# One layer of a fused kernel on one Trainium2 core: the tiles of its second product are put between the steps of its first

## The chip, the cores and the metric

The kernel runs on one core of one Trainium2 chip. The metric is the device time of one execution in microseconds (us). The time given for a kernel is the median of several executions; beside it there is one profiled execution, from which all rows below come. TensorE (PE) multiplies matrices, ScalarE (ACT) and VectorE (DVE) work element by element, and SyncE (SP) issues the DMAs.

## The reference

```python
attn = softmax(mask(q @ k.T / 8))  @ v      # window of 64, 4 x 8 heads, 576 x 64
x = attn as [2304, 512]
h = relu(x @ w_in1);  x2  = h * h @ w_out1            # layer 1: 512 -> 2048 -> 512
h = x2 @ w_in2;       out = (h * cos(h)) @ w_out2     # layer 2: 512 -> 2048 -> 512
```

All is float32. The change concerns layer 2 alone: 2304 tokens, h of width 2048, then the second product back to 512.

## The kernel before

**Numbers.** A float32 operand is kept as a high and a low part, and each product is three matmuls (high by high, high by low, low by high). One step of 128 x 128 weights is therefore three matmuls in a row.

**Layer 2.** The tokens are taken in three pairs (`p` = 0, 1, 2) of two halves of 384 tokens (`half` 0 and 1). The first product, h = x2 @ w_in2, is done for both halves at once with seven block products in place of eight (a form of Strassen's scheme, of Winograd's kind), in eight **groups** (`jp` = 0 to 7) per pair. A group gives four slices of h: `2jp` and `2jp+1` of half 0 and the same of half 1. The seven products of a group (`product`, L997) have six matmuls of 384 columns each, and go in this order, with the PSUM bank that they fill: B11 (x), B21 (y), T2 (x), T1 (z), T3 (x), T4 (x), B22 (z). The bank x is one buffer that all four x products of a group reuse. After B11, T2 and T3, ACT copies the bank to SBUF (`hold`, L1013) before the next x product may overwrite it; after T4 the bank is read in place. DVE adds a held copy to y or z (`add`, L1020), which gives a slice of h in SBUF (`keep`).

**h * cos(h)** (`act2`, L891 to L908) is done for each of the four slices of a group, named a and b (half 0) and c and d (half 1): ACT, three DVE steps, a sine on ACT, one DVE product. `split2` (L929 on DVE, a copy on ACT) parts the result into high and low (`gb`); for half 1 it is done later, tile `gb_e`.

**The second product** is cut into jobs, one for each slice `k` = 0 to 15 of a half (`Job`, `tile_op`, L955). A job has three **tiles** (m = 0, 1, 2: 128 tokens each) of three matmuls of 512 columns, which add into one PSUM bank per m (`accB`). There are four such banks, so the three of one half and one of the other fit. With the last slice a tile's sum is complete; ACT or DVE copies it to `o` (L969, L971; two buffers, ring `x2`) and SP stores it (L975).

**The order on PE** is written out by hand: `line` chains every PE step to the one before. The jobs of half 0 fill the next group: `fill[0]` is the job of slice `2jp-2`, `fill[1]` that of `2jp-1`. In a group, one tile stands between T3 and T4, two between T4 and B22, three after B22. In the first group of pair 0 the fill is two steps of layer 1's second product, of four tiles each (`g2`). After the eight groups come jobs 14 and 15 of half 0, then the jobs of half 1; the last two of them fill the first group of the next pair, except in the last pair, where all 16 run to the end, slice by slice.

**The order on the other engines** comes from a planner (`Plan.run`), which knows for each operation a cost, a key (smaller goes first) and a latency to its readers (`lat`), goes through a model of time and fixes one static order per engine. On the chip each engine takes its instructions in that order and waits where an input is not there yet. The planner's costs are no instruction of the kernel.

Of the kernel before, what the change touches and what calls it, by code (L numbers as in the profile page):

```python
# [13 lines left out]
AF = mybir.ActivationFunctionType  # L14
# [71 lines left out]
class Plan:  # L86
# [6 lines left out]
    def op(self, engs, key, fn, deps=(), take=(), use=(), lat=None):  # L93
        if lat is None:
            lat = self.PE_LAT if "PE" in engs else self.LAT
        o = Op(engs, key, fn, [d for d in deps if d is not None], list(take), lat)
        o.seq = len(self.ops)
        self.ops.append(o)
        for b in (*take, *use):
            b.users.append(o)  # L100
        return o
# [61 lines left out]
def act_us(n, sbuf=True):  # L163
    return 0.05 + 0.093 * sbuf + n / 1200.0
# [15 lines left out]
def kernel(  # L180
# [16 lines left out]
    nc = tc.nc  # L197
    NT = out.shape[0]
    NJ = w1.shape[0]
# [3 lines left out]
    NCC = 4  # L203
    DM = 512
    UA = 256
    H = 384
# [22 lines left out]
    op = plan.op  # L229
# [431 lines left out]
    class UnitA:  # L661
# [47 lines left out]
        def g2(self, j, m, t, w):  # L709
            i, k = divmod(m, self.per)  # L710
            if j == 0 and k == 0 and self.n > 0:
                self.acc[i] = ps_acc.tile(
                    [P, self.per, self.w], F32, tag="acc", name=f"accA_{self.n}_{i}")
            for p, (wl, gl) in enumerate(((0, 0), (0, 1), (1, 0))):
                nc.tensor.matmul(  # L715
                    self.acc[i][:, k, :], w[:, 1, wl, m * P:m * P + P], t["g"][:, gl, :],
                    start=(j == 0 and p == 0 and k == 0 and self.n > 0),
                    stop=(j == NJ - 1 and p == 2 and k == self.per - 1), skip_group_check=True)
# [262 lines left out]
    rest = {}  # L981

    def group(p, jp, key, fill):

        pa, pb = w_in[p, jp]
        bx, by, bz = R["ph"].buf(), R["at"].buf(), R["at"].buf()
        ps = {}

        def product(bank, buf, src, i, o, first, last, deps=()):
            wb, o_w = src  # L990
            for c in range(2):
                def mm(e, c=c):
                    if first and c == 0:
                        pool, tag = (ps_ph, "ph") if bank == "x" else (ps_at, "at")
                        ps[bank] = pool.tile([P, H], F32, tag=tag, name=f"{bank}_{p}_{jp}")
                    for k, (wl, xl) in enumerate(((0, 0), (0, 1), (1, 0))):
                        nc.tensor.matmul(  # L997
                            ps[bank], wb.tile[:, i, wl, c * P:c * P + P], piece(o, c, xl),
                            start=(first and c == 0 and k == 0),
                            stop=(last and c == 1 and k == 2), skip_group_check=True)  # L1000

                new = first and c == 0
                line[0] = op({"PE": 3 * pe_us(H)}, key, mm,
                             [line[0], o_w, *piece_ready[p, o, c], *(deps if c == 0 else ())],
                             [buf] if new else [],
                             [wb] if new else [wb, buf], lat=0.0 if c == 0 else None)
            if jp == NJP - 1:
                piece_used[p, o] = line[0]
            return line[0]

        def hold(buf, bank, dep):
            b = R["R"].buf()
            return b, op({"ACT": act_us(H, False)}, key - 6, lambda e: nc.scalar.activation(  # L1013
                r_at(b), ps[bank], AF.Copy), [dep, o_rooms], [b], [buf])

        def r_at(b):
            return l2["r"][b.slot // 2][:, (b.slot % 2) * DM:(b.slot % 2) * DM + H]

        def add(dst, take, use, bank, buf, r, deps):
            return op({"DVE": dve_us(H)}, key - 6, lambda e: nc.vector.tensor_tensor(  # L1020
                dst(), ps[bank], r_at(r), ALU.add), deps, take, [*use, buf, r])

        nm = f"{p}_{jp}"
        o = product("x", bx, pa, 0, B11, True, True)
        r1, o_r1 = hold(bx, "x", o)
        o = product("y", by, pa, 1, B21, True, True)
        hb = R["h"].buf()
        ap, take, use = room(16)
        h11 = lambda: (ap(), keep[3].tile[:, (1 + hb.slot) * H:(2 + hb.slot) * H])[1]
        o_h = add(h11, [*take, hb], use, "y", by, r1, [o, o_r1])  # L1030
        rest[p, 0, 2 * jp] = act2(key + 0.4, h11, [hb, keep[3]], o_h, f"a{nm}", True)

        o = product("x", bx, pa, 2, T2, False, True, [o_r1])
        r2, o_r2 = hold(bx, "x", o)
        oz = product("z", bz, pa, 3, T1, True, True)
        o = product("x", bx, pb, 0, T3, False, True, [o_r2])
        r3, o_r3 = hold(bx, "x", o)
        k22 = 2 * jp + 1
        ap22, take, use = room(k22)
        o_22 = add(ap22, take, use, "z", bz, r3, [oz, o_r3])  # L1040
        rest[p, 1, k22] = (act2(job_at(p, k22) - 3.0, ap22, use or take, o_22, f"d{nm}", True,
                                ap22), ap22, use or take)
        fill[0][0]()
        o = product("x", bx, pb, 1, T4, False, True, [o_r3])
        rest[p, 0, 2 * jp + 1] = act2(key + 1.2, lambda: ps["x"], [bx], o, f"b{nm}", False)
        for f in fill[0][1:]:
            f()
        o = product("z", bz, pb, 2, B22, False, True, [o_22])
        k12 = 2 * jp
        ap12, take, use = room(k12)  # L1050
        o_12 = add(ap12, take, use, "z", bz, r2, [o, o_r2])
        rest[p, 1, k12] = (act2(job_at(p, k12) - 3.0, ap12, use or take, o_12, f"c{nm}", True,
                                ap12), ap12, use or take)
        for f in fill[1]:
            f()

    def job_at(p, k):
        return base + p * 22.7 + 16.8 + 0.376 * (2 + k)
# [15 lines left out]
    NA = len(items)  # L1074
    place += [2.0 * NJ + k for k in range(NA - len(place))]
    base = place[-1] - LAG + 1.0
    N2 = NJ + J0
    att_at = {0: [1], N2 - 4: [2], N2: [3, 4]}
    for s in range(2, NSA - 1):
        n, k = spans[s + 1]  # L1080
# [28 lines left out]
                g1_last[n] = line[0]  # L1109
        return u.act(lambda: t["ph"], phb, str(i), key + 0.5, line[0])  # L1110

    def g2(i, key, g):
        u, j = items[i]
        t, gb, ready = g
        wb = w_buf[j]
        ends = []
        for m in range(u.groups):
            def mm(e, m=m):
                u.g2(j, m, t, wb.tile)

            take, use = u.g2_bufs(j, m)
            line[0] = op({"PE": u.group_us}, key + 0.5 + m / 8, mm,
                         [line[0], w_hi[j][1], w_lo[j][1], *ready], take, [gb, wb, *use],
                         lat=None if j == NJ - 1 else 0.0)
            ends.append(line[0])
        if j == NJ - 1:
            u.finish(key - 4.0, ends)


# [5 lines left out]
    gs = {}  # L1135
# [39 lines left out]
    for jp in range(2):  # L1175
        load_in(0, jp, base - 10.0 + 2.0 * jp, [gate, *w2_end])
    load_out(0, base - 7.0, [gate, *w2_end])
    fills = [[lambda i=i: g2(i, base, gs.pop(i))] for i in (NA - 2, NA - 1)]
    job_ends = []

    def job(p, half, k):
        key = job_at(p, k) if half else base + p * 22.7 + 2.1 * (k // 2 + 1)
        if half:
            o, ap, use = rest[p, 1, k]
            g = split2(key - 1.5, ap, use, [o, *job_ends[-3:-2]], f"e{p}_{k}", k % 2 == 0)
        else:
            g = rest[p, 0, k]
        j = Job(p, half, k, g)

        def one(m):  # L1190
            j.tile_op(m, key)
            if m == 2:
                job_ends.append(line[0])

        return [lambda m=m: one(m) for m in range(3)]

    for p in range(NPAIR):
        ends = []
        for jp in range(NJP):
            if jp:  # L1200
                fills = [job(p, 0, 2 * jp - 2), job(p, 0, 2 * jp - 1)]
            key = base + p * 22.7 + 2.1 * jp
            if jp >= 2:
                load_in(p, jp, key - 4.2, [ends[jp - 2]])
            if not p and jp:
                load_out(jp, key - 2.1, [ends[jp - 2]] if jp >= 2 else [gate, *w2_end])
            group(p, jp, key, fills)
            ends.append(line[0])
        for k in (NJ - 2, NJ - 1):
            for f in job(p, 0, k):  # L1210
                f()
        last = p == NPAIR - 1
        if not last:
            prepare(p + 1, base + (p + 1) * 22.7 - 1.5, [line[0]])
        for k in range(NJ if last else NJ - 2):
            if k == 2 and not last:
                for jp in range(2):
                    load_in(p + 1, jp, base + (p + 1) * 22.7 - 4.0, [line[0]])
            for f in job(p, 1, k):
                f()  # L1220
        if not last:
            fills = [job(p, 1, NJ - 2), job(p, 1, NJ - 1)]

# [65 lines left out]
```

## Time and profile before

| | |
|---|---|
| median of 3 runs | 883.48 us (882.9 to 885.95) |
| profiled execution | 882.73 us, its span 881.0 us |
| PE, DVE, ACT busy | 849.1, 583.0, 526.0 us |
| instructions | 13894 |

The span goes from the first to the last instruction; the profiled execution is 1.73 us longer than its span. Attention and layer 1 take the first 483 us. Layer 2 follows: the groups of the three pairs lie at about 483 to 581, 614 to 710 and 743 to 839 us, with the jobs of half 1 behind each of them. A matmul's shown length is longer than the distance to the next one, as they overlap; distances of starts are used below.

### The profile page before, as it was taken

What the parts mean: (1) busy time and instruction counts of PE and PEld (TensorE: products, weight loads), DVE (VectorE), ACT (ScalarE), POOL (GpSimd) and SP (SyncE); (2) the same over time, 40 slices, a digit from 0 to 9 for tenths busy, and PEclk for the clock granted to TensorE, in tenths of its full rate; (3) what the DMA queues carried; (4) which work ended last, traced back from release to release, by engine and by line L of the source; (5) the groups of instructions that cost most, each with busy time, mean ns of one, the idle gap of its engine ahead of it and who ended that gap; (6) DMA issues with size and microseconds to landing.
All of it is one profiled execution on the core that took longest, in us unless ns stands there. A gap on an engine that the chain in (4) does not pass through costs nothing.

```text
span 881.0 us, 13894 instructions
## 1 busy us (share of the span) xinstructions
PE 849.1 (96%) x5232; PEld 729.9 (83%) x5232; DVE 583.0 (66%) x1343; ACT 526.0 (60%) x1103; POOL 5.0 (1%) x25
## 2 busy tenths in 40 slices
PE   5699999999999999999999999999999999999997
PEld 4588778998878888888888889888888888888886
DVE  4977856556646566544712788876888875988841
ACT  6899967656656666646434555553656563655542
POOL 2000000000000000000000000000000000000000
PEclk8899999999999999999999999999999999999999
DMA  8852316535455463543920496043553051742000
GB/s 332 360 232 96 126 52 210 219 121 212 173 199 189 160 251 141 192 176 105 375 85 0 139 420 278 1 142 133 219 199 120 1 210 65 285 169 84 1 36 36
DMA packets 28451, 144.16 MB, mean 164 GB/s; under 512 B 3040, under 2 KB 3552, under 8 KB 18144
## 3 DMA queue, kind: packets, MB, share of 16 engines
q1 hardware_dynamic: 28384, 143.27, 43.2%
q8 instruction: 41, 0.67, 0.3%
q14 instruction: 26, 0.21, 0.1%
HBM read 110.76 MB, written 32.51 MB: 163 GB/s over the span
## 4 chain that ended last, share of the span: by engine, by line
PE 74%; ACT 12%; DVE 10%; issue 2%; DMA 1%; ACTq 0%; DVEq 0%
PE accB L955 20%; PE ph L1099 18%; PE accA L715 18%; PE x L997 6%; PE z L997 3%; PE y L997 3%; PE S L556 2%; PE O L607 2%; PE T L593 2%; ACT u_a L891 2%; ACT u_a L905 2%; DVE keep L1020 2%; DVE rr_a L895 2%; DVE rr_a L898 2%; ACT raw_in_w_dram L249 1%
## 5 line engine op out<-in xcount | busy, mean ns | idle before, releaser
L1099 PE MATMUL ph<-X,W_in_w_dram 128*128 128x512 f32 (+1 forms) x1032 | 220.7, 360 | 2.8 <-ACT X L643 1.3
L715 PE MATMUL accA<-g,W_in_w_dram 128*128 128x512 f32 (+1 forms) x888 | 199.7, 370 | 0.2 <-DVE g L701 0.2
L1099 PEld LDWEIGHTS ph<-X,W_in_w_dram 128*128 128x128 f32 x1032 | 171.6, 190 | 32.3 <-issue 1.5
L715 PEld LDWEIGHTS accA<-g,W_in_w_dram 128*128 128x128 f32 x888 | 153.5, 189 | 27.9 <-issue 0.7
L701 DVE TENSOR_TENSOR g<-r,g 128x512 fp32r<-128x512 f32 (+1 forms) x86 | 51.8, 604 | 117.5 <-ACT r L696 117.1
L955 PE MATMUL accB<-wo,gb_e 128*128 128x512 f32 x432 | 99.6, 389 | 0.0
L955 PEld LDWEIGHTS accB<-wo,gb_e 128*128 128x128 f32 x432 | 81.0, 188 | 16.5
L692 ACT ACTIVATE g<-r 128x512 fp32r<-128x512 f32 (+1 forms) x86 | 48.2, 561 | 72.6 <-PE accA L715 71.9
L688 ACT ACTIVATE r<-ph 128x512 f32<-128x512 f32 (+1 forms) x86 | 45.0, 523 | 52.0 <-PE ph L1099 49.6
L575 ACT ACTIVATE pb<-pb,mm 128x128 f32<-128x128 f32 x144 | 55.9, 394 | 11.7 <-DVE mm L569 11.5
L955 PE MATMUL accB<-wo,gb_a 128*128 128x512 f32 x216 | 57.2, 393 | 0.0
L955 PE MATMUL accB<-wo,gb_b 128*128 128x512 f32 x216 | 53.7, 393 | 0.0
L997 PE MATMUL x<-X,wb 128*128 128x384 f32 x216 | 47.9, 347 | 5.1 <-ACT held L1013 5.1
L997 PEld LDWEIGHTS x<-X,wb 128*128 128x128 f32 x216 | 36.9, 188 | 15.3 <-ACT held L1013 15.2
L696 ACT ACTIVATE r<-r 128x512 f32<-128x512 f32 (+1 forms) x84 | 47.1, 561 | 2.6
L1013 ACT ACTIVATE held<-x 128x384 f32<-128x384 f32 x72 | 34.4, 478 | 21.1 <-PE x L997 20.8
L997 PE MATMUL x<-X,wa 128*128 128x384 f32 x216 | 45.9, 338 | 1.0 <-ACT held L1013 1.0
L955 PEld LDWEIGHTS accB<-wo,gb_b 128*128 128x128 f32 x216 | 40.2, 188 | 7.4
L955 PEld LDWEIGHTS accB<-wo,gb_a 128*128 128x128 f32 x216 | 40.0, 188 | 5.6
L929 DVE TENSOR_TENSOR gb_e<-keep,gb_e 128x384 fp32r<-128x384 f32 x48 | 26.0, 555 | 27.0 <-ACT gb_e L249 27.0
L905 ACT ACTIVATE u_b<-rr_b,hpi 128x384 f32<-128x384 f32 x24 | 14.8, 618 | 46.7 <-DVE rr_b L901 46.7
L997 PEld LDWEIGHTS x<-X,wa 128*128 128x128 f32 x216 | 38.7, 188 | 3.4 <-ACT held L1013 1.3
(123 smaller groups left out, 1279.6 us busy)
## 6 DMA issues: line engine op xcount, KB each, us to landing
raw_in_w_dram<-in_w_dram SPq DMA_DIRECT2D x32, 1024.0 KB, 5.9
wa<-w2a_dram SPq DMA_DIRECT2D x24, 1024.0 KB, 8.7
wb<-w2b_dram SPq DMA_DIRECT2D x24, 768.0 KB, 8.0
qk<-in_qk_dram SPq DMA_DIRECT2D x18, 576.0 KB, 4.3
v<-in_v_dram SPq DMA_DIRECT2D x18, 512.0 KB, 3.6
w2o_dram<-w2o SPq DMA_DIRECT2D x8, 1024.0 KB, 4.2
w2a_dram<-w2a SPq DMA_DIRECT2D x8, 1024.0 KB, 4.5
wo<-w2o_dram SPq DMA_DIRECT2D x8, 1024.0 KB, 12.2
```

Source lines behind the costliest of these rows:

```text
L575: nc.scalar.activation(t["pb"][:, e, r, i], t["pb"][:, e, r, i], AF.Exp, bias=t["mm"][:, e, r, i:i + 1], scale=-1.0, accum_out=t["sm"][:, ...
L688: nc.scalar.activation(t["r"], ph()[:, 0:w], AF.Relu)
L692: nc.scalar.activation(t["g"][:, 0], t["r"], AF.Square)
L696: nc.scalar.activation(t["r"], t["r"], AF.Square)
L701: nc.vector.tensor_tensor(t["g"][:, 1], t["r"], f32(t["g"][:, 0]), ALU.subtract)
L715: nc.tensor.matmul(self.acc[i][:, k, :], w[:, 1, wl, m * P:m * P + P], t["g"][:, gl, :], start=(j == 0 and p == 0 and k == 0 and self.n > ...
L905: nc.scalar.activation(f32(t["u"]), t["r"], AF.Sin, bias=hpi)
L929: nc.vector.tensor_tensor(t["g"][:, 1], r(), f32(t["g"][:, 0]), ALU.subtract)
L955: nc.tensor.matmul(acc[0], t["g"][:, gl, m * P:m * P + P], wb.tile[:, k % 2, wl], start=(k == 0 and i == 0), stop=(k == NJ - 1 and i == 2))
L997: nc.tensor.matmul(ps[bank], wb.tile[:, i, wl, c * P:c * P + P], piece(o, c, xl), start=(first and c == 0 and k == 0), stop=(last and c == ...
L1013: return b, op({"ACT": act_us(H, False)}, key - 6, lambda e: nc.scalar.activation(r_at(b), ps[bank], AF.Copy), [dep, o_rooms], [b], [buf])
L1099: nc.tensor.matmul(t["ph"][:, 0:u.w], wb.tile[:, 0, wl, c * P:c * P + P], u.x(xl, c), start=(c == 0 and k == 0), stop=(c == NCC - 1 and k ...
```

## The change

It is on layer 2 alone. The six tiles that fill a group are spread: one before T2, one between T1 and T3, two between T3 and T4, one between T4 and B22, the last (in the very first group, which has eight tiles, the last three) after B22. `g2` can be called for single tiles for that. The first tile (m = 0) of the jobs 0 and 1 of half 1 goes ahead of jobs 14 and 15 of half 0, and the point from which their `split2` may go is named by the `split2` of jobs 14 and 13 of half 0. In the last pair the last three slices of half 1 are done by m: slices 13, 14, 15 for m = 0, then for m = 1, then for m = 2. In the planner, `hold` gets a longer cost and a latency of 0.39 us.

```diff
         def hold(buf, bank, dep):
             b = R["R"].buf()
-            return b, op({"ACT": act_us(H, False)}, key - 6, lambda e: nc.scalar.activation(
-                r_at(b), ps[bank], AF.Copy), [dep, o_rooms], [b], [buf])
+            return b, op({"ACT": act_us(H)}, key - 6, lambda e: nc.scalar.activation(
+                r_at(b), ps[bank], AF.Copy), [dep, o_rooms], [b], [buf], lat=0.39)
...
+        tiles = [*fill[0], *fill[1]]
+        gaps = [tiles[0:1], tiles[1:2], tiles[2:4], tiles[4:5], tiles[5:]]
+
+        def between():
+            for f in gaps.pop(0):
+                f()
+
+        between()
         o = product("x", bx, pa, 2, T2, False, True, [o_r1])
         r2, o_r2 = hold(bx, "x", o)
         oz = product("z", bz, pa, 3, T1, True, True)
+        between()
         o = product("x", bx, pb, 0, T3, False, True, [o_r2])
...
-        fill[0][0]()
+        between()
         o = product("x", bx, pb, 1, T4, False, True, [o_r3])
...
-        for f in fill[0][1:]:
-            f()
+        between()
         o = product("z", bz, pb, 2, B22, False, True, [o_22])
...
-        for f in fill[1]:
-            f()
+        between()
...
-            g = split2(key - 1.5, ap, use, [o, *job_ends[-3:-2]], f"e{p}_{k}", k % 2 == 0)
+            after = job_ends[-3:-2] if k > 1 else [rest[p, 0, NJ - 2 - k][2][0]]
+            g = split2(key - 1.5, ap, use, [o, *after], f"e{p}_{k}", k % 2 == 0)
...
+        ahead = [job(p, 1, k) for k in range(2)]
+        for k in range(2):
+            ahead[k].pop(0)()
         for k in (NJ - 2, NJ - 1):
             for f in job(p, 0, k):
                 f()
...
-        for k in range(NJ if last else NJ - 2):
+        for k in range(NJ - 3 if last else NJ - 2):
...
-            for f in job(p, 1, k):
+            for f in ahead[k] if k < 2 else job(p, 1, k):
                 f()
+        if last:
+            tail = [job(p, 1, k) for k in range(NJ - 3, NJ)]
+            for m in range(3):
+                for fs in tail:
+                    fs[m]()
```

## Rows read from the trace of the kernel before

**Rows 1.** Stretches: us, busy PE, PEld, DVE, ACT, POOL; PE's clock, DMA share, GB/s.
```profile
509.62:569.48 59.86, 58.78 (x301) 53.09 (x301) 52.31 (x106) 34.62 (x66) 0.00 (x0) 1.00 0.58 236
585.38:612.00 26.62, 26.62 (x119) 22.06 (x118) 19.04 (x40) 11.70 (x26) 0.00 (x0) 1.00 0.60 227
```

**Rows 2.** PE's waits (us, times, longest): whole span, then pair 2's groups.
```profile
PE x L997 <- ACT held L1013: 6.1, 24, 1.0
...
PE x L997 <- ACT held L1013: 1.8, 8, 0.3
```

**Rows 3.** Timeline of PE, one group of pair 0 (start, length, what).
```profile
521.44 1.23 PE L997 MATMUL x<-X,wa 128*128 128x384 f32 x6
522.50 1.20 PE L997 MATMUL y<-X,wa 128*128 128x384 f32 x6
...
524.58 1.20 PE L997 MATMUL z<-x_more,wa 128*128 128x384 f32 x6
525.62 0.68 PE L997 MATMUL x<-x_more,wb 128*128 128x384 f32 x3
...
526.66 0.86 PE L955 MATMUL accB<-wo,gb_a 128*128 128x512 f32 x3
527.74 1.31 PE L997 MATMUL x<-X,wb 128*128 128x384 f32 x6 [0.21 <-ACT held L1013]
528.88 1.55 PE L955 MATMUL accB<-wo,gb_a 128*128 128x512 f32 x6
530.27 1.21 PE L997 MATMUL z<-X,wb 128*128 128x384 f32 x6
531.32 2.24 PE L955 MATMUL accB<-wo,gb_b 128*128 128x512 f32 x9
533.40 1.23 PE L997 MATMUL x<-X,wa 128*128 128x384 f32 x6
```

**Rows 4.** Timeline of PE's weight loads, T4 of that group.
```profile
527.73 0.99 PEld L997 LDWEIGHTS x<-X,wb 128*128 128x128 f32 x6 [0.65 <-ACT held L1013]
```

**Rows 5.** Timeline of ACT, that group.
```profile
526.69 0.62 ACT L905 ACTIVATE u_a<-rr_a,hpi 128x384 f32<-128x384 f32 x1 [1.29 <-DVE rr_a L901]
527.21 0.47 ACT L1013 ACTIVATE held<-x 128x384 f32<-128x384 f32 x1
```

**Rows 6.** Timeline of DVE, that group.
```profile
523.81 0.56 DVE L1020 TENSOR_TENSOR keep<-y,held 128x384 f32<-128x384 f32 x1 [0.18 <-PE y L997]
...
527.34 0.56 DVE L908 TENSOR_TENSOR rr_a<-keep,u_a 128x384 f32<-128x384 f32 x1 [0.74 <-ACT u_a L905]
```

**Rows 7.** Timelines of PE and ACT, second group of pair 0.
```profile
496.83 1.21 PE L997 MATMUL y<-X,wa 128*128 128x384 f32 x6
499.00 0.79 PE L997 MATMUL x<-X,wa 128*128 128x384 f32 x3 [0.96 <-ACT held L1013]
...
501.48 0.79 PE L997 MATMUL x<-x_more,wb 128*128 128x384 f32 x3
...
498.04 0.52 ACT L249 ACTIVATE gb_b<-rr_b 128x384 fp32r<-128x384 f32 x1 [0.85 <-DVE rr_b L908]
498.47 0.47 ACT L1013 ACTIVATE held<-x 128x384 f32<-128x384 f32 x1
```

**Rows 8.** Timelines of PE and DVE, end of pair 0's groups.
```profile
576.78 1.56 PE L955 MATMUL accB<-wo,gb_a 128*128 128x512 f32 x6
...
583.34 2.20 PE L955 MATMUL accB<-wo,gb_b 128*128 128x512 f32 x9
...
581.44 0.56 DVE L929 TENSOR_TENSOR gb_b<-rr_b,gb_b 128x384 fp32r<-128x384 f32 x1
```

**Rows 9.** Timeline of the kernel's end.
```profile
873.93 1.52 PE L955 MATMUL accB<-wo,gb_e 128*128 128x512 f32 x6
874.13 1.28 ACT L969 ACTIVATE o<-accB 128x512 f32<-128x512 f32 x2 [6.27 <-PE accB L955]
...
876.93 0.60 ACT L969 ACTIVATE o<-accB 128x512 f32<-128x512 f32 x1 [1.52 <-DMA out_dram<-o]
```

More of the change, by code (lines that the diff above doesn't have):

```diff
@@ L1110, in g1, with g2 @@
         return u.act(lambda: t["ph"], phb, str(i), key + 0.5, line[0])
-    def g2(i, key, g):
+    def g2(i, key, g, ends=None, part=None):
         u, j = items[i]
@@ L1115, in g2 @@
         wb = w_buf[j]
-        ends = []
-        for m in range(u.groups):
+        ends = [] if ends is None else ends
+        for m in range(u.groups) if part is None else part:
             def mm(e, m=m):
@@ L1125, in g2 @@
             ends.append(line[0])
-        if j == NJ - 1:
+        if j == NJ - 1 and len(ends) == u.groups:
             u.finish(key - 4.0, ends)
@@ L1177 @@
     load_out(0, base - 7.0, [gate, *w2_end])
-    fills = [[lambda i=i: g2(i, base, gs.pop(i))] for i in (NA - 2, NA - 1)]
+    fills = []
+    for i in (NA - 2, NA - 1):
+        g, ends = gs.pop(i), []
+        fills.append([
+            lambda i=i, g=g, ends=ends, m=m: g2(i, base, g, ends, [m]) for m in range(NCC)])
     job_ends = []
```

## The prediction

> **What bounds the kernel now.** First the busy time by stretch, to see which engine a stretch belongs to. Among the jobs of half 1 PE is busy for the whole of it, 26.62 of 26.62 us, at a granted clock of 1.00 [rows 1]: nothing is to be had there by another order. Over five groups PE is busy 58.78 of 59.86 us at the same clock, and DVE 52.31 [rows 1]; so PE leads, but some time leaks, and DVE is a close second. Then PE's waits: everything that PE waits for in layer 2 is one thing, the x product behind a `hold`, 6.1 us in 24 waits, 8 of them (1.8 us) in pair 2 [rows 2]. As a busy PE is not a PE at its peak, the last view is the timeline of one group, read by starts.
>
> B11 takes 522.50 - 521.44 = 1.06 us and T1 525.62 - 524.58 = 1.04; six matmuls of 512 columns take 530.27 - 528.88 = 1.39, so a tile of three takes 0.69 [rows 3]. T3's tile starts at 526.66, so T4 could start at 527.35; it starts at 527.74, 0.39 later, and then takes 528.88 - 527.74 = 1.14 instead of 1.04 [rows 3]. One wait thus costs 0.39 + 0.10 = 0.49, although the view of waits shows 0.21. The reason lies on ACT: the copy after T3 stands behind the sine of slice a, which waits for DVE; it starts at 527.21 and ends at 527.68, and T4 starts right after [rows 5].
>
> The extra 0.10 is the restart: T4's weight load also began only with the release, after an idle time of 0.65 us [rows 4]. The Trainium skill (page "TensorE: Matmul & The Clock Gate", Part 2, step 1) has the queue pull weight loads ahead of running matmuls; by it a wait would cost its own 0.39 alone, and the gain below would be 23 x 0.10 = 2.3 us smaller. This case's row speaks against that at a wait, and the sum goes by the row.
>
> A group lasts 533.40 - 521.44 = 11.96 us [rows 3]; without the wait it would be 11.47.
>
> **The change, part by part.** It adds and removes no instruction: the same matmuls, copies and DMAs are put in another order. The planner's new cost and latency of `hold` are not executed; they can only move ACT's and DVE's order.
>
> *T4's cover.* Between T3 and T4 there are now two tiles, 1.39 us, in place of 0.69. T4 comes due 0.70 later, and the wait was 0.39, so it is gone with 0.3 to spare if ACT keeps its order and its times. 23 of the 24 groups have this wait (the first had twelve matmuls between; the 24th wait is another, next): 23 x 0.49 = 11.3 us gained. T2 and T3 get a tile of 0.69 each as cover that they did not have.
>
> *The second group of pair 0.* T2 should start at 496.83 + 1.04 = 497.87 and starts at 499.00, 1.13 late, since the `hold` stood on ACT behind `gb_b`, itself late for DVE [rows 7]. T2 and T1 then take 501.48 - 499.00 = 2.48 instead of 2.08 [rows 7]. The new tile covers 0.69 of the first, and the tile before T3 most of what lies in the second (0.27 of the 0.40; the rest is the restart, which stays). Gained: 0.69 + 0.27 = 0.96.
>
> *The end of the kernel.* PE's last matmul ends at 875.45; the third copy starts at 876.93, 1.48 later, as it waits for the store that empties one of two output buffers [rows 9]. Done by m, the first sum is complete six tiles (4.1 us) before the last and the second three before it, so both stores have begun long before, and the first has ended. Copy and store of the last follow as before. Gained: 1.45. Its price would be a late `gb_e` of slices 14 and 15, wanted 2 to 3 us earlier; their `split2` may go from the end of job 10 on, and PE waits nowhere among these jobs now, so I take nothing.
>
> *Two tiles ahead.* There was no wait at that place, so by themselves they gain nothing. They pay for the later T4: `gb_b` is complete at 581.44 + 0.56 = 582.00, which is 5.22 us after T4's end at 576.78, and job 15, which needs it, starts at 583.34 [rows 8]. After the change there lie between T4's end and job 15 one tile, B22, one tile, the two tiles ahead and job 14 (583.34 less 2.04 is its start): 0.69 + 1.04 + 0.69 + 1.39 + 2.04 = 5.85 us. That leaves 0.63. The `split2` of the tiles ahead come before it on DVE at worst, 2 x 0.56 = 1.12: then PE waits 0.49 and restarts for 0.10. Bounds 0 and 0.6 for each of three pairs; I take 0.2, 0.6 in all, since DVE has a hole of 0.74 in each group [rows 6] in which one of the two fits. Also moved: the first tile ahead uses the fourth sum bank, free as before, the tiles behind job 15 one that ACT has to copy out first; a copy takes 1.28 / 2 = 0.64 [rows 9] and has 1.39, so nothing.
>
> *DVE, now nearer.* This is the unknown price. With the wait gone PE wants a group each 11.47 us. DVE waits 0.18 for PE in a group, and 0.74 for the sine of slice a [rows 6]. If all its waits for ACT stay, DVE cannot go round in less than 11.96 - 0.18 = 11.78; if the sine's wait is filled with another slice's steps, in 11.04. PE's 11.47 lies between. A DVE that is late first uses up the slack of the copies, so the loss per group lies between 0 and 0.31, and 0 to 7.1 in 23 groups. I take 0.05, 1.2 in all, nearer to nothing: four of the six tiles now stand before T4, so slices b and c come later in a group, and their DVE steps fall into the time in which a's sine runs. DVE holds up ACT, and ACT `hold`: that is who waits.
>
> *Moved past queues.* SP: in the first group of pairs 1 and 2 the three stores of half 1 come as their tiles end, spread over the group; loads of weights queue behind them, but for a group that is one to two groups ahead. The finishing copies of layer 1 stay behind the last fill. No cost taken.
>
> **Sum.** Gains 11.3 + 0.96 + 1.45 = 13.7; prices 0.6 + 1.2 = 1.8; net 11.9 us. The profiled execution took 882.73 (span 881.0 and 1.73 around it), so 870.8; the median of the runs is 0.75 higher, 883.48, which gives 871.6 for a median.
>
> **Rivals.**
>
> *DVE becomes the bound (0.18).* All DVE waits stay, a group takes 11.78. The gain per group is 0.18, 23 x 0.18 = 4.1, with 0.96 + 1.45 - 0.6 it is 5.9: 877.6. For it: DVE's busy 52.31 of 59.86 us, with records missing (106 of 110 steps) [rows 1], and a planner that cannot know the chip's lateness. Against it: the tiles' new places shift b and c as above, and lateness must pile up group by group while each pair begins with DVE free.
>
> *No change (0.06).* DVE's order comes out with more waits, at 11.9 or above, and only the end is gained: 882.
>
> *A copy falls behind two late ACT steps (0.06), slower.* The place is the `hold` after B11 or T2, in each group. The second group of pair 0 shows the mechanism: one late step cost T2 1.13 + 0.13 us [rows 7]. With 0.69 of cover it would cost 0.44 + 0.13 there. It decides when PE's wait with its restart passes 13.7 / 23 = 0.60 a group, that is when the copy ends about 1.04 + 0.69 + 0.5 = 2.2 us after its product; two steps of 0.62 with a DVE wait between do that. At a wait of 0.9: 23 x (0.9 + 0.1) - 13.7 = 9.3 us slower, 892.8. Against it: only one of 24 groups shows one such step, in the stretch where layer 1's last copies are still under way.
>
> **Chances and range.** The forecast has 0.70: 869.0 (no price at all, 883.48 - 13.7 = 869.8, less part of the 0.75 by which executions differ) to 874.5 (both prices doubled and the 0.75). A measurement of this kernel can tell about 0.3%, 2.65 us, from no change. Forecast and first rival lie beyond it: faster 0.88, same 0.06, slower 0.06. The range of 868.8 to 879.0 takes in the first rival.
>
> **What would show it.** In the changed kernel's waits PE no longer waits for `hold` in groups, or by under 0.1 each; groups start every 11.5 us; the end shows the third copy right behind PE's last matmul. The forecast is wrong if group starts lie 11.7 or more apart with DVE's waits for PE gone; if PE waits for `gb_b` at job 15; or if T2 or T3 shows the wait that T4 lost.

## The result and the profile after

| | before | after |
|---|---|---|
| median, first comparison | 883.37 us (4 runs, 882.9 to 885.95) | 872.04 us (4 runs, 869.96 to 873.25) |
| ratio, 95% interval | | 0.9854, 0.9828 to 0.988 |
| median, second comparison | 884.36 us (11 runs, 882.72 to 886.56) | 871.78 us (6 runs, 869.37 to 874.42) |
| ratio, 95% interval | | 0.986, 0.9838 to 0.9883 |
| profiled execution: span | 881.0 us | 871.1 us |
| from the first B21 to the end of the span | 397.0 us | 383.8 us |

The change made the kernel 11.3 us faster in the first comparison and 12.6 us in the second, by the medians; 871.6 was forecast. (The ratio is the one on record beside its interval, not the quotient of the two medians, which is 0.987 and lies in the interval too. Both intervals leave 1 out.) The last line of the table is the measure used from here on. B21 (the bank y) is the second product of a group and easy to find; its first start is at 483.94 before and at 487.30 after, and what lies ahead of it is attention and layer 1, which the change leaves alone. Over all profiled executions here, of whatever kernel, that first start lies anywhere between 483.80 and 487.34. The rest of the span repeats closely: 383.84 and 383.85 in two profiled executions of the changed kernel. So of the 9.9 us between the two spans, layer 2 gave 13.2, and the start of that execution took 3.4 back; the last section shows that such differences of the start do not go with the kernel.

The busy time of five groups after the change (length, busy PE, weight loads, DVE, ACT, POOL, then PE's clock, DMA's share and GB/s):

```profile
511.79:569.55 57.76, 57.76 (x302) 53.71 (x301) 49.40 (x105) 33.45 (x65) 0.00 (x0) 1.00 0.58 233
```

Five groups lasted 59.86 us [rows 1]; they last 57.76 now, and PE is busy for all of it. PE's waits in the whole span have no row of layer 2 left; these are the shortest two, where [rows 2] had 6.1 us for the x products:

```profile
PE ph L1106 <- DVE X L646: 0.3, 1, 0.3
PE accA L715 <- DVE g L701: 0.2, 1, 0.2
```

A group on PE's timeline, to be read against [rows 3]:

```profile
522.28 1.22 PE L997 MATMUL x<-X,wa 128*128 128x384 f32 x6
523.34 1.20 PE L997 MATMUL y<-X,wa 128*128 128x384 f32 x6
524.38 0.86 PE L955 MATMUL accB<-wo,gb_a 128*128 128x512 f32 x3
525.08 0.69 PE L997 MATMUL x<-X,wa 128*128 128x384 f32 x3
...
528.94 0.86 PE L955 MATMUL accB<-wo,gb_a 128*128 128x512 f32 x3
529.64 0.85 PE L955 MATMUL accB<-wo,gb_b 128*128 128x512 f32 x3
530.33 1.20 PE L997 MATMUL x<-X,wb 128*128 128x384 f32 x6
531.37 0.86 PE L955 MATMUL accB<-wo,gb_b 128*128 128x512 f32 x3
...
533.83 1.05 PE L997 MATMUL x<-X,wa 128*128 128x384 f32 x5
```

T4 starts at 530.33, when its two tiles are through, and takes 531.37 - 530.33 = 1.04: neither wait nor restart. The copy that it needs, on ACT, is not earlier than before, seen from T3:

```profile
529.14 0.53 ACT L249 ACTIVATE gb_a<-rr_a 128x384 fp32r<-128x384 f32 x1
529.58 0.47 ACT L1013 ACTIVATE held<-x 128x384 f32<-128x384 f32 x1
```

It starts 529.58 - 528.94 = 0.64 after the first tile behind T3, where it was 527.21 - 526.66 = 0.55 [rows 3, 5], and ends at 530.05, 0.28 before T4. The group takes 533.83 - 522.28 = 11.55, where the forecast had 11.47. A lone tile takes 525.08 - 524.38 = 0.70, B11 behind a tile 1.06 and B21 behind a product 1.04.

At the end of pair 0's groups (DVE, then PE) `gb_b` is complete at 583.15, 0.31 before job 15 wants it; [rows 8] had 1.34:

```profile
582.59 0.56 DVE L929 TENSOR_TENSOR gb_b<-rr_b,gb_b 128x384 fp32r<-128x384 f32 x1
...
583.46 2.20 PE L955 MATMUL accB<-wo,gb_b 128*128 128x512 f32 x9
```

At the end of the kernel the third copy starts 0.08 behind PE's last matmul, 861.76 + 5.38 = 867.14, instead of 1.48 behind it [rows 9]:

```profile
861.76 5.38 PE L955 MATMUL accB<-wo,gb_e 128*128 128x512 f32 x23
...
863.09 0.60 ACT L969 ACTIVATE o<-accB 128x512 f32<-128x512 f32 x1 [3.56 <-PE accB L955]
...
867.22 0.60 ACT L969 ACTIVATE o<-accB 128x512 f32<-128x512 f32 x1 [1.49 <-PE accB L955]
```

### The profile page after: what moved, and what is told of

The parts are those of the page before. It is cut to its first block, busy times and chain, and to the rows that moved or that the text cites. A ratio compares the mean times of both kernels' runs of the same rounds, so it can differ in the third digit from the quotient of the medians.

```text
span 871.1 us, 13901 instructions
## 1 busy us (share of the span) xinstructions
PE 847.9 (97%) x5232; PEld 737.2 (85%) x5232; DVE 572.3 (66%) x1345; ACT 522.9 (60%) x1101; POOL 5.0 (1%) x25
## 4 chain that ended last, share of the span: by engine, by line
PE 91%; DVE 4%; ACT 3%; DMA 1%; issue 0%; ACTq 0%; DVEq 0%
PE accB L955 23%; PE ph L1106 21%; PE accA L715 19%; PE x L997 12%; PE z L997 6%; PE y L997 3%; PE S L556 2%; PE O L607 2%; PE accA L776 2%; PE T L593 2%; ACT pb L575 1%; DMA w2o_dram<-w2o 1%; ACT raw_in_w_dram L286 0%; DVE pb L585 0%; DVE xr L820 0%; DMA qk<-in_qk_dram 0%
## 5 line engine op out<-in xcount | busy, mean ns | idle before, releaser
L1106 PE MATMUL ph<-X,W_in_w_dram 128*128 128x512 f32 (+1 forms) x1032 | 223.0, 363 | 2.7 <-ACT X L643 1.4
L1106 PEld LDWEIGHTS ph<-X,W_in_w_dram 128*128 128x128 f32 x1032 | 173.7, 193 | 32.5 <-issue 1.5
L955 PE MATMUL accB<-wo,gb_a 128*128 128x512 f32 x216 | 60.8, 394 | 0.0
L955 PE MATMUL accB<-wo,gb_b 128*128 128x512 f32 x216 | 60.6, 393 | 0.0
L997 PE MATMUL x<-X,wb 128*128 128x384 f32 x216 | 45.5, 336 | 0.0
L997 PEld LDWEIGHTS x<-X,wb 128*128 128x128 f32 x216 | 38.9, 188 | 2.2
## 6 DMA issues: line engine op xcount, KB each, us to landing
wo<-w2o_dram SPq DMA_DIRECT2D x8, 1024.0 KB, 11.8
```

The lines of the kernel that those rows point to most:

```text
L955: nc.tensor.matmul(acc[0], t["g"][:, gl, m * P:m * P + P], wb.tile[:, k % 2, wl], start=(k == 0 and i == 0), stop=(k == NJ - 1 and i == 2))
L997: nc.tensor.matmul(ps[bank], wb.tile[:, i, wl, c * P:c * P + P], piece(o, c, xl), start=(first and c == 0 and k == 0), stop=(last and c == ...
L1106: nc.tensor.matmul(t["ph"][:, 0:u.w], wb.tile[:, 0, wl, c * P:c * P + P], u.x(xl, c), start=(c == 0 and k == 0), stop=(c == NCC - 1 and k ...
```

## The experiments

The table gives, for each kernel's profiled execution, the distance between starts of B21 in the later groups of a pair, the time from the first B21 to the end, and that from PE's last matmul to the end, all in us.

| kernel | group | first B21 to end | last matmul to end |
|---|---|---|---|
| before | 11.97 | 397.0 | 5.50 |
| after | 11.55 | 383.8 | 4.00 |
| e1_tail_only | 11.99 | 396.0 | 4.12 |
| e2_cover_only | 11.76 | 391.8 | 5.51 |
| e3_old_hold_cost | 12.07 | 393.5 | 4.00 |
| e4_none_ahead | 11.55 | 385.6 | 3.89 |
| e5_three_gaps | 11.81 | 389.4 | 4.11 |
| e6_new_hold_cost_only | 11.99 | 398.6 | 5.39 |
| e7_clamp_b_twice | 11.72 | 386.6 | 3.99 |
| e8_four_gaps | 11.60 | 385.2 | 4.00 |
| e9_three_gaps_dve_cost | 11.59 | 385.3 | 4.00 |
| e10_changed_again | 11.55 | 383.9 | 3.99 |
| e11_three_before_t4 | 11.53 | 384.0 | 4.00 |
| e12_two_gaps | 11.49 | 383.1 | 4.00 |

**The end alone** (e1_tail_only), on the kernel before:

```diff
-        for k in range(NJ if last else NJ - 2):
+        for k in range(NJ - 3 if last else NJ - 2):
...
+        if last:
+            tail = [job(p, 1, k) for k in range(NJ - 3, NJ)]
+            for m in range(3):
+                for fs in tail:
+                    fs[m]()
```

> The kernel before, with nothing changed but the last three slices of the last pair, which are done by m. Measured from the first B21 of layer 2 to the span's end (397.0 us before, 383.8 after). Theory (the third copy waited for an output buffer): 1.45 us shorter, 395.6, the third copy starting within 0.1 of PE's last matmul instead of 1.48 behind it, groups as before at 11.97. Rival (the stores themselves set the end): no change, 397.0.

The end went from 5.50 to 4.12 us. The whole came to 396.0 in place of 395.6, since the groups took 0.02 more in that execution. The third copy had waited for a buffer, as the theory has it; the rival, by which nothing would change, is out.

**The cover of T4 alone** (e2_cover_only), on the kernel before:

```diff
-        fill[0][0]()
+        tiles = [*fill[0], *fill[1]]
+        early = 2 if len(tiles) == 6 else 1
+        for f in tiles[:early]:
+            f()
         o = product("x", bx, pb, 1, T4, False, True, [o_r3])
...
-        for f in fill[0][1:]:
-            f()
+        for f in tiles[2:3] if early == 2 else []:
+            f()
...
-        for f in fill[1]:
-            f()
+        for f in tiles[3:] if early == 2 else tiles[1:]:
+            f()
```

> The kernel before, with two tiles before T4 and one before B22 in place of one and two; no tile before T2 or T3, none ahead, the end and the planner as before. Theory (T4's missing cover is the whole loss of a group, and DVE has room): PE no longer waits for the copy, groups start every 11.47 us (even less than the 11.55 after, as PE changes between widths less often), 11 us shorter: 386. Rival (DVE goes round in 11.78 in this order, and the spread of the tiles is what helps): PE waits again, groups at 11.7 to 11.8, only 4 to 5 us shorter: 392.

The rival's numbers came, 11.76 and 391.8, though T4 has its cover. PE now loses at T3:

```profile
547.29 1.21 PE L997 MATMUL z<-x_more,wa 128*128 128x384 f32 x6
548.47 0.79 PE L997 MATMUL x<-x_more,wb 128*128 128x384 f32 x3
549.10 0.70 PE L997 MATMUL x<-X,wb 128*128 128x384 f32 x3
```

T3 starts 548.47 - 547.29 = 1.18 after T1 in place of 1.04, and its first three matmuls take 549.10 - 548.47 = 0.63 in place of 0.52: a wait of 0.14 that the view of waits leaves out, and a restart. T3 needs the copy after T2, which ACT starts only at 547.95, behind two steps of `act2`, the first of which waits for DVE. The steps on DVE, from a group's B21 on:

```profile
545.88 0.55 DVE L898 SCALAR_TENSOR_TENSOR rr_c<-u_c,rr_c 128x384 f32<-128x384 int32 x1
546.46 0.36 DVE L901 TENSOR_SCALAR rr_c<-rr_c 128x384 f32<-128x384 f32 x1
546.74 0.55 DVE L1020 TENSOR_TENSOR keep<-y,held 128x384 f32<-128x384 f32 x1
547.57 0.56 DVE L908 TENSOR_TENSOR keep<-keep,u_c 128x384 f32<-128x384 f32 x1 [0.28 <-ACT u_c L905]
548.08 0.56 DVE L895 SCALAR_TENSOR_TENSOR rr_a<-u_a,keep 128x384 f32<-128x384 int32 x1
...
550.36 0.56 DVE L908 TENSOR_TENSOR rr_a<-keep,u_a 128x384 f32<-128x384 f32 x1 [0.74 <-ACT u_a L905]
```

DVE waits for c's sine, 0.28, and for a's, 0.74, one after the other, and it no longer waits for PE: the addition of y starts 0.2 later in a group than before (B21's first start plus 1.53, against 523.81 - 522.50 = 1.31 [rows 3, 6]). The two sines on ACT have each waited for DVE:

```profile
546.92 0.62 ACT L905 ACTIVATE u_c<-rr_c,hpi 128x384 f32<-128x384 f32 x1 [1.02 <-DVE rr_c L901]
...
549.72 0.62 ACT L905 ACTIVATE u_a<-rr_a,hpi 128x384 f32<-128x384 f32 x1 [1.30 <-DVE rr_a L901]
```

So DVE and ACT wait for each other in a circle, and the circle is longer than PE's own group, which is 11.50 in the first group of pairs 1 and 2 here. The addition of y is a good sign of it: 1.31 after B21's first start it comes as soon as the bank y is complete, and any later start means that DVE, or the copy that it adds, is late.

**The planner's old figures** (e3_old_hold_cost), on the changed kernel:

```diff
-            return b, op({"ACT": act_us(H)}, key - 6, lambda e: nc.scalar.activation(
-                r_at(b), ps[bank], AF.Copy), [dep, o_rooms], [b], [buf], lat=0.39)
+            return b, op({"ACT": act_us(H, False)}, key - 6, lambda e: nc.scalar.activation(
+                r_at(b), ps[bank], AF.Copy), [dep, o_rooms], [b], [buf])
```

> The changed kernel, with the planner's old cost and latency for the copies. Theory (the tiles' places do it): no waits of PE in the groups, 11.55 a group, 383.8 us from the first B21 to the end. Rival (the planner's new figures keep the copies in front of late steps on ACT): waits of 0.1 to 0.4 with a restart of 0.1 come back at T2, T3 or T4 of most groups, 388 to 395.

The theory was wrong. With the new places and the old figures a group takes 12.07, more than the 11.97 before, and 9.6 of the 13.2 us are lost. DVE's order is another. First this kernel's, then the changed kernel's, both from the end of one group into the next:

```profile
557.63 0.56 DVE L895 SCALAR_TENSOR_TENSOR rr_c<-u_c,keep 128x384 f32<-128x384 int32 x1 [0.22 <-ACT u_c L891]
558.22 0.56 DVE L898 SCALAR_TENSOR_TENSOR rr_c<-u_c,rr_c 128x384 f32<-128x384 int32 x1
558.70 0.55 DVE L1020 TENSOR_TENSOR keep<-y,held 128x384 f32<-128x384 f32 x1
...
563.38 0.56 DVE L929 TENSOR_TENSOR gb_a<-rr_a,gb_a 128x384 fp32r<-128x384 f32 x1 [0.59 <-ACT gb_a L249]
...
565.09 0.56 DVE L895 SCALAR_TENSOR_TENSOR rr_d<-u_d,keep 128x384 f32<-128x384 int32 x1 [0.68 <-ACT u_d L891]
```

```profile
524.75 0.55 DVE L1020 TENSOR_TENSOR keep<-y,held 128x384 f32<-128x384 f32 x1
525.21 0.55 DVE L895 SCALAR_TENSOR_TENSOR rr_c<-u_c,keep 128x384 f32<-128x384 int32 x1
525.80 0.56 DVE L898 SCALAR_TENSOR_TENSOR rr_c<-u_c,rr_c 128x384 f32<-128x384 int32 x1
526.27 0.55 DVE L895 SCALAR_TENSOR_TENSOR rr_a<-u_a,keep 128x384 f32<-128x384 int32 x1
...
528.55 0.56 DVE L908 TENSOR_TENSOR rr_a<-keep,u_a 128x384 f32<-128x384 f32 x1 [0.47 <-ACT u_a L905]
```

With the old figures the addition of y stands behind two steps of slice c, which wait for ACT, and starts 558.70 - 556.37 = 2.33 after B21's first start. With the new ones it goes ahead of them, at 524.75 - 523.34 = 1.41 (1.31 in 22 of the 24 groups), and a's and c's steps are interleaved, so that part of each wait is filled. Two covers then fall short in e3: T3 and T4 both wait, 0.20 and 0.12 in that group. Why the new figures put the addition ahead of c is a matter of the planner's model and was not followed step by step; the cost and the latency were always changed together.

**The planner's new figures alone** (e6_new_hold_cost_only): the reverse of that edit, on the kernel before.

> The kernel before with nothing but the planner's new cost and latency for the copies. Theory (places and figures are needed together): at best T4's copy starts right after T3, 0.07 after its last matmul's end, and T4 still waits 0.05 to 0.1 and restarts for 0.1; DVE's loop of 11.78 stays, so 11.75 to 11.97 a group and 391 to 397. Rival (the figures alone order ACT rightly): under 11.6 a group, 388.

398.6, 1.6 more than before and just above the 391 to 397 expected; PE waits 7.5 us in 26 waits. Ordinary groups take 11.99, and the second group of each pair, with 14.07 and twice 12.73 in place of 13.69, 12.20 and 12.23, takes most of the loss. Neither half of the change does it. The places give 3.6 of 13.2 (e3), and 3.6 is what the second group of pair 0 (13.69 to 11.55 in e3 too) and the end (5.50 to 4.00) come to there: the other groups together gained nothing. The figures alone lose.

**No tiles ahead** (e4_none_ahead), on the changed kernel:

```diff
-        ahead = [job(p, 1, k) for k in range(2)]
-        for k in range(2):
-            ahead[k].pop(0)()
...
-            for f in ahead[k] if k < 2 else job(p, 1, k):
+            for f in job(p, 1, k):
```

The named point for `split2` of slices 0 and 1 went back to the old one with it.

> The changed kernel, without the two tiles of half 1 ahead of jobs 14 and 15. Theory (they cover the later T4): after the change gb_b was complete 0.3 us before job 15 needed it, with two tiles (1.38 us) in front; without them, and with one split2 less before it, PE waits 0.6 to 1.1 us at job 15 of each pair and restarts for 0.1: 2 to 3.5 us longer, 386 to 387. Rival (the planner moves gb_b forward, nothing was needed): 383.8.

1.8 us longer. PE's timeline, job 14 and job 15 of half 0:

```profile
578.32 2.22 PE L955 MATMUL accB<-wo,gb_a 128*128 128x512 f32 x9
580.67 2.47 PE L955 MATMUL accB<-wo,gb_b 128*128 128x512 f32 x9
582.98 3.33 PE L955 MATMUL accB<-wo,gb_e 128*128 128x512 f32 x14
```

Job 15 starts 2.35 after job 14 in place of 2.04, and itself takes 582.98 - 580.67 = 2.31: 0.6 lost per pair, 1.7 in three. The tiles ahead, with their named point, are needed, for a little less than I expected; the view of waits shows one wait of 0.2 for all of it.

**DVE's room** (e7_clamp_b_twice), on the changed kernel, in `act2`:

```diff
-            nc.vector.tensor_scalar(
-                t["r"], t["r"], -PI_IN - HALF_PI, PI_IN - HALF_PI, ALU.max, ALU.min)
+            for _ in range(2 if nm[0] == "b" else 1):
+                nc.vector.tensor_scalar(
+                    t["r"], t["r"], -PI_IN - HALF_PI, PI_IN - HALF_PI, ALU.max, ALU.min)
```

> The changed kernel with the clamp of slice b (a DVE step that gives the same values when done twice) issued twice: 0.28 to 0.31 us more DVE work in each group, the planner's order unchanged. Theory (after the change DVE's loop is just inside PE's group, with under 0.1 to spare): groups lengthen by 0.2 to 0.3, to about 11.8, with PE waiting for copies again, 383.8 + 24 x 0.25 = 390. Rival (DVE has the 1.1 us of its waits as room): 11.55 a group, 384.

The first three or four groups of a pair stay at 11.55; then they lengthen to 11.72, and layer 2 takes 2.8 us more. The clamps of b and d on DVE, in this kernel and in the changed one:

```profile
659.61 0.74 DVE L902 TENSOR_SCALAR rr_b<-rr_b 128x384 f32<-128x384 f32 x2
660.27 0.35 DVE L902 TENSOR_SCALAR rr_d<-rr_d 128x384 f32<-128x384 f32 x1
```

```profile
534.01 0.35 DVE L901 TENSOR_SCALAR rr_b<-rr_b 128x384 f32<-128x384 f32 x1
534.27 0.35 DVE L901 TENSOR_SCALAR rr_d<-rr_d 128x384 f32<-128x384 f32 x1
```

From b's clamp to d's it is 0.66 in place of 0.26, so the edit added about 0.4 to a group, not the 0.28 to 0.31 expected. The group grew by 0.17. By estimate DVE's circle has 0.4 - 0.17, some 0.2 us, of room inside PE's group, if all of the added time lies in the circle, and not the 1.1 of its waits. Lateness does pile up first, as the prediction had it: in pair 1 the addition of y starts 1.31, 1.33, 1.39, 1.57 and then 1.75 after B21, and the fifth group is the first that is longer.

**Fewer gaps** (e5_three_gaps and e8_four_gaps), on the changed kernel:

```diff
-        gaps = [tiles[0:1], tiles[1:2], tiles[2:4], tiles[4:5], tiles[5:]]
+        gaps = [tiles[0:0], tiles[0:0], tiles[0:2], tiles[2:3], tiles[3:]]   # e5
+        gaps = [tiles[0:0], tiles[0:1], tiles[1:3], tiles[3:4], tiles[4:]]   # e8
```

> The changed kernel with its tiles in three gaps in place of five: none before T2 and T3, two before T4, one before B22, three after it; the end, the two tiles ahead and the planner's new figures as after. Theory now (the group is a loop through DVE and ACT, whose length their static order sets; the five gaps with the new figures gave an order that fits into PE's 11.55): the order that comes out here has slice c's sine and a's sine each waited for by DVE, as before, so groups start every 11.75, as with the cover alone, and the first B21 to the end takes 390. Rival (the cover of T4 and the planner's figures are enough): PE does not wait, 11.47 a group, 382.

> The changed kernel with its tiles in four gaps: none before T2, one before T3, two before T4, one before B22, two after it. Theory: one change of width less for PE (0.04), and an order of DVE in which a and c are interleaved as after; if its loop fits, 11.51 a group and 383; if the order puts more waits for sines into DVE's loop, 11.6 to 11.8 and 385 to 390, with PE's waits at T2 or T3. Rival (the number of gaps is what counts, each cover by itself): T2 waits in every group for its copy, 0.2 or more.

Three gaps: 11.81, DVE once more behind c's sine (0.28) and a's (0.74), and the addition of y 1.6 after B21, as the theory of the circle has it. Four gaps: 11.51 in the first group of pairs 1 and 2, 11.60 in most later ones. The view of waits has one wait for all of layer 2, yet T2 loses time in the later groups (PE, then the copy after B11 on ACT):

```profile
670.20 0.77 PE L997 MATMUL x<-X,wa 128*128 128x384 f32 x3
670.82 0.68 PE L997 MATMUL x<-x_more,wa 128*128 128x384 f32 x3
...
669.66 0.47 ACT L1013 ACTIVATE held<-x 128x384 f32<-128x384 f32 x1
```

The copy ends at 670.13, hardly before T2, and T2's first three matmuls take 670.82 - 670.20 = 0.62 (0.61 before rounding) in place of 0.52. That restart is all of 11.60 - 11.51. So the rival, by which T2 pays for having no cover, is right in kind here, at less than its 0.2. DVE is late in these groups too, with the addition of y 1.69 after B21; this run alone does not part the two.

**Three gaps and a longer DVE cost** (e9_three_gaps_dve_cost), on e5: the planner's cost of each DVE step in `act2`, `split2` and `add` is 0.05 longer.

> The kernel with three gaps (none before T2 and T3, two tiles before T4, one before B22, three after), and in addition the planner counts each DVE step of layer 2 0.05 us longer (0.515 for 384 columns, nearer to the distance of starts of about 0.48 to 0.59 in the traces). The instructions are those of the run with three gaps, only their static order may differ. Theory (the order on DVE and ACT decides, not the number of covers): with a better order PE waits nowhere, groups start every 11.47 (PE changes widths as seldom as in the kernel before), 11.81 less 0.34 in 20 groups, and the first B21 to the end takes 382, 1.5 to 2 less than after the change. Rival (T2 and T3 need their own covers, whatever the order): groups stay at 11.75 to 11.85, 389.

The same instructions and places as e5, another order, 11.59 instead of 11.81, and no wait of PE in the later groups. DVE has room now, as this step, the addition of y, shows:

```profile
648.00 0.56 DVE L1023 TENSOR_TENSOR keep<-y,held 128x384 f32<-128x384 f32 x1 [0.86 <-PE y L1000]
```

The addition comes 1.31 after B21 in every group. So the order decides, not the covers of T2 and T3: neither has one here. But it is 11.59, not 11.47, and layer 2 took 385.3, not 382; the first group of pair 0 alone cost 14.0 in place of 12.94. PE's timeline of the same group shows what the other groups lose:

```profile
650.85 1.55 PE L958 MATMUL accB<-wo,gb_a 128*128 128x512 f32 x6
652.24 1.31 PE L1000 MATMUL x<-X,wb 128*128 128x384 f32 x6
653.39 0.87 PE L958 MATMUL accB<-wo,gb_a 128*128 128x512 f32 x3
```

T4 starts on time, 1.39 behind its tiles, but takes 1.15. It pays the restart without a wait of PE; the weight loads show why, first here, then in the changed kernel:

```profile
652.21 1.01 PEld L1000 LDWEIGHTS x<-X,wb 128*128 128x128 f32 x6 [0.25 <-ACT held L1016]
```

```profile
530.10 1.11 PEld L997 LDWEIGHTS x<-X,wb 128*128 128x128 f32 x6
```

T4's first load begins 0.03 before T4 here, held back until the copy is done, and 0.23 before it in the changed kernel.

**The changed kernel again** (e10_changed_again):

> The changed kernel itself, timed beside the kernel before and the one with three gaps and the longer DVE cost. Its layer 2 should take 383.8 again, from the first B21 to the end, within 0.3; its whole time lies 11 to 13 us under the kernel before on the same chip, with attention and layer 1 varying by some 3 us from run to run in either. If the difference of 13.2 in layer 2 is the change's effect and the rest chance, the mean gain over more runs moves from 11.3 toward 13; if attention and layer 1 are really slower after, it stays at 10 to 11.5.

Layer 2 took 383.9; the medians differ by 12.6. That goes toward the 13.2 of layer 2, but the interval, 10.3 to 14.3 us, holds 11.3 and 13.2 alike; the medians do not decide it.

**Three tiles before T4, and two gaps** (e11_three_before_t4 and e12_two_gaps), on e9:

```diff
-        gaps = [tiles[0:0], tiles[0:0], tiles[0:2], tiles[2:3], tiles[3:]]
+        gaps = [tiles[0:0], tiles[0:0], tiles[0:3], tiles[3:4], tiles[4:]]   # e11
+        gaps = [tiles[0:0], tiles[0:0], tiles[0:3], [], tiles[3:]]           # e12, DVE cost + 0.07
```

> The run before with three gaps and the longer DVE cost, with three tiles before T4 in place of two (none before T2 and T3, three before T4, one before B22, two after it). There PE waited nowhere by the view of waits and a group still took 11.59: T4's second matmul came 0.26 after its first in place of 0.17, so the copy came just in time and the restart's 0.10 stayed. Theory (a wait too short for the view costs the whole restart; each change of width costs about 0.02 to 0.04): with 0.69 more cover the 0.10 goes, groups at 11.47 to 11.50, the first B21 to the end 382 to 382.5, some 1.5 under the changed kernel. Rival (something else makes the 262 ns, such as reading the bank behind the copy): 11.59 stays, 385.

> The same with the tiles in two gaps alone, three before T4 and three after B22 (DVE steps counted 0.07 us longer by the planner, which gives an order of the same kind). B22 then follows T4 at once, and its bank needs DVE's addition of T1. Theory (changes of width cost 0.04 a pair, and DVE's loop still fits): 11.43 to 11.46 a group, 381 to 382. Rival (the addition comes too late for B22, or DVE's loop is longer than PE's 11.45): a wait at B22 and 11.6 or more, 385 or more.

With three tiles the restart at T4 is gone, and a group takes 11.50 in the first two of pairs 1 and 2, then 11.53: most of the 0.10 was that. Two gaps give 11.49, and with it the shortest layer 2 of all, 383.1, 0.8 below the changed kernel; timed, its ratio to the kernel before is 0.9848 (0.9823 to 0.9872) against 0.986 (0.9838 to 0.9883), which the runs cannot tell apart. Both expectations were 1 to 2 us too low. Some 0.6 of it is the start of pair 0, whose first two groups took 13.3 and 11.8, where the changed kernel had 12.94 and 11.55; the rest is 0.03 to 0.06 in each group.

## Why the prediction was right

**T4's cover.** The wait and its restart are gone in every group, as forecast, for 23 x 0.49 = 11.3 us. Measured: the first two groups of pair 0 apart, the other 22 came down by 0.44 each on average, 10.0 in all with 0.42 for that second group. (The second groups of pairs 1 and 2 are in it with 0.65 and 0.68; they had stood at 12.20 and 12.23, which the sum did not see.) The difference is a price that the sum did not have, below. The step said that the cover does it "if ACT keeps its order and its times", and gave the planner's new figures no weight of their own. This was the weak step. ACT did not keep its order: before, the copy after T3 stood right behind a's sine, and now c's sine and `gb_a` are between them. With these places and the old figures the order turned against PE (e3, 12.07 a group), and the cover alone gives 11.76 (e2). That the copy still came 0.28 before T4, where the forecast had 0.3, is the work of cover and new figures together; the prediction had no reason for the second half, and on that point it was lucky.

**The new places' price on PE.** Each lone tile takes 0.70 in place of 0.69, and each product behind a tile 1.06 in place of 1.04. Five gaps give 11.55, three 11.50, two 11.49 where PE waits for nothing (e11, e12). The forecast took 11.47 for a group without a wait. 24 x 0.08 = 1.9 us were mis-sized here: 0.05 a group for the two gaps more, and 0.03 in the reading of the group before, where T4's 1.14 was held against T1's 1.04, though a product behind a tile takes 1.06, so that less of it was restart.

**DVE.** Taken: 1.2, with bounds of 0 and 7.1. Measured: 0, PE waits nowhere. The reason given, that steps of b and c would fall into the time of a's sine, is not what the rows show: DVE still waits 0.47 for a's sine, and only c's clamp stands in that time. With the same places and the old figures, DVE is 1 us late. What made the price 0 is the order that came with the new figures. The first rival's mechanism is real all the same: it came about in e2 at 11.76, against the 11.78 of the forecast, and e7 shows that the changed kernel passes it by some 0.2 us a group.

**The phase ends.** Taken: 0.6; measured: 0, with 0.31 to spare where the forecast had 0.63 less up to 1.12. The tiles ahead with their named point are worth 1.8 us (e4).

**The second group of pair 0.** Taken: 0.96; measured: 13.69 to 11.55, that is 2.14, of which 0.42 are T4's. T2's wait went altogether, not only the 0.69 that the tile covers. The places alone do this (11.55 in e3 too).

**The end.** Taken: 1.45; measured: 5.50 - 4.00 = 1.50, and 1.38 alone (e1).

Together: 10.0 + 1.7 + 1.5 = 13.2 in layer 2, against 13.7 less 1.8 = 11.9. T4's term was 1.3 too high; the second group gave 0.7 more than the sum had, and the two prices, 1.8 together, did not come. So the errors cancelled in part. That the first median came within 0.4 us of 871.6 is chance on top: layer 2 gained 1.3 more than forecast, and the starts of the kernel differ by more than that. The last rival, a copy behind late steps, did not come; e3 shows its mechanism, with waits at T3 and T4 and a DVE that is 1 us late, yet it ended 3.6 us under the kernel before and not above.

## What to carry to other kernels

Where engines go through static orders, find the circle: follow one group's chain through all engines back to itself and compare its length with the busy engine's time for a group. Cover for a wait helps only as far as the next longest circle, and the planner's cost and latency of a step can decide what the place of the covering work is worth (in the new places they made 9.6 of 13.2 us, in the old ones they lost 1.6). Test a moved order with the planner's old figures and the old order with the new ones before crediting either. Read a wait by the starts of the steps behind it, since the view of waits showed 0.21 of 0.49, and in two kernels nothing of 0.09.

## What was not expected of the hardware

A wait too short for the view still costs the restart: in e9 T4 took 1.15 in place of 1.06 in a group without any wait of PE. Its first weight load had been held back until the copy was done, 0.25 us by the timeline of the loads. The Trainium skill (page "TensorE: Matmul & The Clock Gate", Part 2, step 1) says that the queue pulls weight loads ahead of running matmuls; the changed kernel's row agrees, with T4's load 0.23 us before T4, and in e11, with more cover, T4 took 1.07. In e9 no such pull was seen for the load that goes with a matmul that still has something to wait for.

A change of width costs PE a little: with tiles of 512 columns alone between products of 384 it is 0.70 and 1.06 against 0.69 and 1.04, about 0.02 us for each gap.

The start of the kernel varies by some 3 us between executions. In the stretch from 42 to 60 us, first before, then after, with the columns of [rows 1]:

```profile
42.00:60.00 18.00, 15.63 (x147) 14.98 (x148) 14.04 (x19) 17.78 (x30) 0.00 (x0) 1.00 0.83 332
```

```profile
42.00:60.00 18.00, 14.99 (x118) 14.26 (x119) 12.47 (x19) 15.76 (x26) 0.00 (x0) 0.81 0.79 308
```

The granted clock was 1.00 (2.4 GHz) in the one and 0.81 on average in the other, that is at 1.2 GHz for a part of it, and PE got through 118 matmuls in place of 147. PE had been busy 3.2 and 3.3 of the 5 us from 40 on in the two, hardly different. All fourteen profiled executions fall in line: where the clock of this stretch is 1.00 (seven of them, the kernel before, e2, e3, e6, e8, e9 and e12), the first B21 starts at 483.80 to 484.48; where it is 0.91 (e1, e4, e5, e7 and e10), at 485.39 to 486.51; where it is 0.81 (the changed kernel and e11), at 487.30 and 487.34. So the 3.4 us between the two profiles go with the clock of this stretch, and not with the kernel: the changed kernel itself had 0.81 once and 0.91 once. The clock from 0 to 42 us gives no such order (0.84 before and 0.92 after). For the timed runs without a profile the record has the mean clock of the whole span alone, which does not order their times (869.42 and 874.42 both at 0.992 in the second comparison).
